# A new hand-written order of issue for the first batch of an attention + gated-product kernel

## Chip, cores and metric

The kernel runs on one core of one Trainium2 chip. The metric is the device time of one execution in microseconds (us); smaller is better. Times are compared between runs of whole programs on the same chip.

## What is computed

Attention over 4 batches, 8 heads, 768 positions and head width 64, with a hash mask, followed by a gated product with three weight matrices. In short:

```python
q_bits = (q @ proj > 0); k_bits = (k @ proj > 0)            # 6 bits each
mask   = bucket(q_bits)[:, :, :, None] == bucket(k_bits)[:, :, None, :]
scores = where(mask, q @ k.T / 8, -1e9)
attn   = exp(scores - max) / (sum(exp) + 1e-9)
x      = (attn @ v)  ->  3072 tokens x 512
out    = ((x @ w_a) * (x @ w_b)) @ w_out                    # 512 -> 1536 -> 512
```

## The kernel before

The numbers keep close to float32 although TensorE is fed float16: each operand is scaled and split into a high and a low float16 part, and products are made of three of the four parts.

**Units.** The work is cut by batch (4), by chunk of 256 query rows (3 per batch), and by half (4 heads each). A unit has 8 query tiles (`qtile`). Each tile is: four score matmuls on TensorE (`scores`, L1004), the row maximum on VectorE (L1016), a width (L1025, VectorE) and a bias (L1032 on ScalarE or L1038 on VectorE), the exponential on ScalarE (L1048), a cast to float16 (L1056 VectorE, L1057 ScalarE or L1058 GpSimd), the residue `e - a` (L1068 GpSimd or L1072 VectorE), a DMA transpose issued by SyncE (L1078), and 18 matmuls with V (`outs`, L1087). After both halves of a chunk the result is normalised, split and turned (`su_end`), and `moe` runs the gated product in 12 blocks: 24 matmuls `ab` (L1285), a copy (L1299), a product (L1307), a cast (L1315 or L1319), a residue (L1327, GpSimd) and 6 matmuls `o` (L1337).

**The first batch** has more to do than the others. While its tiles run, the 9.4 MB of weights are loaded, measured (L617), scaled on ScalarE and packed on VectorE (L540, L548, L555), and split into high and low halves (`hi_lo`: L633 or L634, then L638 on GpSimd or L642 on VectorE). K, Q and V of the batch are scaled and split (`scale_pair`, L734 or L731; `split`, L862 to L883), and some of them are turned by TensorE and evicted (L834, L842, L844).

**The order.** Each operation is a step with a number. For each engine the program order is the order in which the steps stand in one list, `ORDER`, written out by hand; nothing is decided at run time but the waits on semaphores. An engine works through its own steps strictly in that order, and so does SyncE with its DMA issues. A number from 10000 up takes the step in another form, mostly on another engine (the `alt` of the step). A negative number -n stands for n matmuls whose result nobody reads ("warm", L1441, 128x128 by 128x256):

```python
def issue(self, order, fill=None):                          # L367
    for x in order:
        if x < 0:
            fill(-x)
            continue
        which, at = divmod(x, 10000)
        o = self.ops[at]
        (o.alt[which - 1][2] if which else o.fn)()

        for _ in range(n):                                  # in fill(n), L1440
            nc.tensor.matmul(
                warm[0][:, 0, :], lhsT=ident16, rhs=ident16.unsqueeze(1).to_broadcast([P, 2, P]), start=True, stop=True
            )
```

The costs and due times that stand beside the steps are not read when the list is there.

Of the kernel before, what the change touches and what calls it, by code (L numbers as in the profile page):

```python
# [75 lines left out]
def constants():  # L76
# [26 lines left out]
    12, 6, 5, 52, 0, 2, 1, 40, 3, 13, 60, 4, 296, 53, 14, 295, 7, 299, 15, -1, 8, 16, 300, 10017, 273, 41, 19, 277, 9,  # L103
    18, -8, 20, 272, 42, 26, 61, 43, 276, 10, -1, 62, 145, 10021, 11, 411, 63, 64, 410, 45, -6, 22, 66, 309, 23, 159,
    298, -7, 24, 67, 46, 301, 25, 44, 65, 302, 297, 303, -1, 54, 10047, 304, 275, 55, 305, 306, 314, 307, -7, 48, 56,
    308, 57, 49, 274, 58, 279, 313, 59, -7, 50, 10027, 315, 51, 278, 280, 310, -10, 281, 10146, 69, 282, 286, 342,
    283, 147, 78, 70, 346, 290, 341, 148, 284, 345, -3, 28, 425, 149, 29, 30, 150, 68, 71, 79, 31, 151, 80, 72, 10081,
    73, 285, 152, 33, -18, 153, 344, 74, 415, 82, 412, 414, 75, 348, 10160, -3, 87, 154, 83, 88, 76, 355, -3, 96, 84,
    89, 161, 10090, 343, 360, 162, 163, 291, -4, 155, 85, 287, 91, 156, 578, 164, 319, 292, -7, 34, 318, 430, 20092,
    97, 157, 323, 10035, 322, 166, 347, 32, 158, 98, 10099, 189, 100, 349, 93, 413, -9, 36, 416, 350, 417, 77, 288,  # L110
    20101, 94, 351, 167, 418, 579, 37, 102, 352, 419, 38, 10168, 420, 289, 421, 103, 580, 86, 424, 665, 588, 39,
    10165, 10581, 426, 429, -10, 105, 114, 583, 427, 169, 354, 584, 428, 320, 106, 359, 115, -9, 95, 332, 170, 107,
    361, -3, 171, 108, 109, 116, 324, 391, 104, 117, 118, 356, 123, 392, 10110, -1, 132, 431, 387, 293, 388, 10111,
    337, 124, 112, 119, 125, 10126, 133, 127, 325, 294, 120, 311, 422, -18, 190, 134, 10135, 321, 10128, 312, 353,
    121, 136, 191, 141, 192, -9, 199, 10193, 10137, 10129, 316, 200, 201, 138, 130, 194, 393, 326, -9, 113, 432,
    10202, 317, 390, 327, 139, 423, 172, 142, 328, 329, -5, 208, 330, 433, 331, 122, 389, 209, 336, 173, -4, 131, 210,
    333, 10582, 203, 181, 334, 365, 338, -7, 140, 10195, 217, 10335, 369, 211, 212, 218, 368, 196, 339, -5, 585, 174,
    401, 340, -3, 175, 219, 394, 197, 220, 182, 204, 364, 586, 10213, 205, 367, 221, -9, 226, 587, 176, 177, -1, 235,
    214, 179, 183, 227, 143, 357, 228, 180, 229, 230, 358, 184, 206, -9, 198, 236, 244, 237, 10238, 178, 185, 239,
    395, 186, 10187, 378, 188, -6, 253, 10222, 838, 254, 10231, 215, 255, 10223, 383, 144, 232, 406, 224, 10256, 245,  # L120
    -15, 207, 257, 20240, 246, 10247, 371, 248, 233, -3, 589, 370, 241, 10839, 362, -1, 598, 262, 840, 366, 841, -4,
    216, 20249, 590, 250, 372, 242, 599, 591, 10592, 10258, -7, 225, 600, 10601, 10363, 602, 251, 263, 10259, 593, -7,
    234, 843, 10594, 607, 260, 616, 848, 595, 608, -1, 243, 603, 609, 10610, 617, 611, 604, 596, 618, 619, 620, -7,
    252, 612, 625, 10613, 605, 634, 626, 20621, -1, 261, 622, 627, 635, 628, 614, 629, 636, 264, 637, 265, 638, -8,
    597, 630, 925, 643, 266, 631, 623, 639, -3, 606, 644, 652, 842, 632, 645, 646, 647, 10267, 268, 653, 844, 10648,
    -8, 666, 654, 10655, 649, 10640, 656, -1, 269, 667, 661, -1, 373, 270, 615, 668, 374, 10669, 20657, 375, 641, 670,
    -3, 633, 271, 658, 624, 382, 396, 650, 662, 675, 397, 377, 20671, 483, 511, 398, 659, 676, 672, 400, 684, 677,
    484, 678, 405, 379, 679, 384, 435, 485, 685, 693, 20680, 380, 439, 642, 434, 486, 686, 10381, 491, 673, 687, 487,
    688, 694, 488, 490, 438, 385, 402, 702, 399, 695, 386, 492, 489, 10689, 703, 651, 704, 493, 705, 660, 10681, 494,
    497, 696, 697, 495, 376, 682, 10403, 10698, 711, 10690, 706, 498, 404, 663, 691, 707, 712, 845, 449, 436, 496,  # L130
    459, 846, 699, 499, 454, 441, 674, 720, 713, 407, 714, 700, 715, 683, 708, 500, 716, 729, 721, 847, 501, 505, 408,
    722, 664, 717, 730, 692, 458, 731, 504, 462, 10723, 10732, 502, 440, 724, 463, 709, 437, 409, 503, 10725, 442,
    461, 506, 733, 443, 1122, 507, 701, 726, 10508, 718, 514, 738, 444, 445, 446, 448, 739, 509, 447, 515, 727, 20734,
    453, 849, 450, 510, 516, 517, 451, 455, 858, 473, 521, 452, 859, 512, 522, 542, 518, 850, 456, 519, 851, 10513,
    478, 735, 860, 464, 520, 523, 460, 852, 853, 465, 457, 710, 10861, 854, 524, 867, 466, 736, 862, 528, 11123, 855,
    525, 1124, 467, 868, 529, 1125, 526, 869, 468, 863, 719, 1127, 876, 530, 856, 870, 527, 871, 531, 1126, 469, 470,
    532, 1128, 728, 864, 877, 472, 535, 471, 10872, 573, 878, 474, 1098, 737, 879, 880, 865, 885, 873, 482, 536,
    10881, 740, 477, 886, 894, 533, 874, 537, 887, 857, 10882, 475, 534, 538, 883, 888, 10539, 476, 889, 895, 545,
    890, 896, 741, 742, 903, 897, 898, 540, 546, 891, 11099, 904, 866, 746, 1100, 905, 10906, 547, 541, 10743, 892,
    899, 1101, 747, 907, 912, 548, 900, 748, 875, 1102, 549, 552, 543, 10908, 744, 1103, 901, 1129, 909, 913, 914,  # L140
    884, 553, 745, 1130, 915, 916, 550, 544, 910, 926, 1105, 921, 935, 554, 1131, 10917, 551, 555, 927, 918, 560, 928,
    936, 1110, 929, 930, 10556, 893, 922, 833, 931, 557, 559, 937, 919, 479, 938, 939, 944, 10932, 1106, 561, 558,
    940, 10480, 945, 902, 481, 911, 946, 562, 933, 953, 947, 948, 567, 10941, 10949, 566, 10563, 942, 954, 564, 962,
    955, 1104, 10956, 1132, 957, 565, 950, 963, 568, 11111, 920, 569, 971, 964, 10965, 10958, 951, 923, 750, 966, 972,
    570, 749, 973, 924, 974, 571, 975, 10959, 934, 751, 1107, 10967, 1112, 572, 1108, 968, 976, 1113, 1109, 752, 980,
    1114, 977, 756, 1148, 1115, 981, 960, 753, 989, 576, 754, 757, 1133, 577, 574, 952, 982, 10983, 758, 943, 990,
    984, 969, 755, 991, 759, 10985, 10992, 1117, 1149, 978, 993, 986, 10760, 764, 1150, 998, 1118, 763, 999, 1151,
    761, 1134, 1152, 1153, 575, 762, 765, 1135, 10994, 1136, 766, 970, 1138, 995, 1137, 10767, 1158, 1167, 987, 1139,
    770, 1225, 768, 1140, 961, 11116, 771, 1159, 21154, 996, 1168, 1155, 979, 772, 1169, 769, 1160, 11161, 773, 1162,
    1156, 778, 1170, 1171, 21163, 1226, 1119, 774, 988, 11172, 775, 1120, 777, 1164, 1141, 1121, 1227, 1176, 779,  # L150
    1228, 1173, 776, 780, 1165, 1229, 1177, 997, 785, 1178, 11230, 1179, 1174, 1000, 10781, 784, 1001, 782, 1002,
    1157, 786, 783, 1180, 1232, 11181, 1185, 787, 1233, 11231, 1194, 1003, 1093, 1182, 1186, 791, 1006, 1237, 1187,
    788, 1004, 1166, 1183, 792, 789, 11188, 1195, 1189, 1005, 1196, 790, 1007, 1197, 793, 21190, 1198, 1008, 794,
    1203, 798, 11199, 10795, 1204, 796, 1234, 799, 1205, 1200, 1235, 11206, 1184, 1238, 1236, 1207, 1175, 11191, 1142,
    800, 797, 11208, 801, 1192, 1143, 802, 1144, 1209, 1239, 1212, 1146, 1201, 1240, 805, 1241, 803, 1213, 1242, 1210,
    806, 1214, 11215, 1145, 1265, 1216, 1244, 1266, 1147, 807, 1249, 804, 1221, 808, 21217, 1257, 1267, 1193, 809,
    1245, 1218, 1275, 1268, 11269, 812, 1270, 1276, 1243, 1219, 813, 1277, 1284, 11278, 810, 1222, 1279, 11271, 11272,
    1280, 1202, 814, 1285, 1211, 1281, 1273, 1293, 815, 1286, 811, 1250, 1287, 816, 1282, 1288, 1258, 817, 819, 1294,
    21289, 1259, 1295, 11296, 820, 1297, 1260, 1261, 1246, 1298, 1251, 821, 818, 1262, 1263, 822, 823, 1264, 826,
    1247, 824, 1438, 827, 1290, 1252, 1248, 1253, 825, 828, 1299, 1255, 829, 1220, 10830, 1009, 831, 1291, 1223, 1439,  # L160
# [1319 lines left out]
```

## Time and profile before

| what | us |
|---|---|
| median of 3 runs | 923.35 |
| the three runs | 919.8, 923.35, 923.75 |
| span of the profiled execution, first to last instruction | 918.4 |

The page of the profile gives no time for the profiled execution but its span. The runs lie 1.4 to 5.35 us above it; the median lies 4.95 us above.

In the rows further down, PE is TensorE, DVE VectorE, ACT ScalarE, POOL GpSimd, SP SyncE, and SPq the queue from which SyncE issues DMAs. Instructions of one engine can overlap by a little, so that the sum of their durations is somewhat over the engine's busy time.

### The profile page before, as it was taken

The page shows a single profiled execution, that of the slowest core. Times are in us where ns is not written, and L with a number is a line of the kernel's source. Part 1 is how long each engine was busy: PE and PEld are TensorE (multiplying, and loading weights), DVE is VectorE, ACT ScalarE, POOL GpSimd, SP SyncE. Part 2 cuts the span into 40 slices and gives each one's busy share as a digit, 9 for nine tenths or more (in the row PEclk, how much of TensorE's full clock was granted, in tenths as well). Part 3 has the DMA queues.
Part 4 walks back from the last instruction along what each step waited for, and adds up shares of the span by engine and source line. Part 5 has one row for each costly group of instructions (what it writes and reads, how often), then busy time and mean ns, then how long its engine had stood idle before and what let it go on. Part 6 is the DMA issues. An engine that isn't in the chain of part 4 may idle for free.

```text
span 918.4 us, 23592 instructions
## 1 busy us (share of the span) xinstructions
PE 864.2 (94%) x9429; PEld 658.4 (72%) x9429; DVE 681.2 (74%) x1622; ACT 543.9 (59%) x1034; POOL 433.0 (47%) x372
## 2 busy tenths in 40 slices
PE   5667789999999999999999999999999999999998
PEld 4455567667777777777777777777777777777775
DVE  7999999998988778777976757776888863752311
ACT  5989879976554656556645455555566545543222
POOL 1347568745553454453343253573454544462111
PEclk9999999999999999999999999999999999999999
DMA  9799999899999789998969579997899976654000
GB/s 330 222 238 235 191 224 229 163 189 194 175 193 184 144 144 197 185 172 153 176 110 187 107 141 163 151 208 151 154 187 169 156 126 113 130 111 70 1 24 24
DMA packets 435950, 147.40 MB, mean 161 GB/s; under 512 B 407552, under 2 KB 428160, under 8 KB 435840
## 3 DMA queue, kind: packets, MB, share of 16 engines
q1 hardware_dynamic: 435840, 145.89, 81.1%
q8 instruction: 74, 1.21, 0.5%
q14 instruction: 36, 0.29, 0.1%
HBM read 37.85 MB, written 6.29 MB: 48 GB/s over the span
## 4 chain that ended last, share of the span: by engine, by line
PE 73%; DVE 9%; ACT 1%; issue 1%; DMA 1%; SPq 0%; ACTq 0%; DVEq 0%
PE ab L1285 36%; PE o L1337 18%; PE s L1004 10%; PE av L1087 8%; DVE mx L1016 2%; DVE xz L1187 1%; DVE g L1307 1%; DMA at<-a 1%; SPq L823 0%; PE b_k L795 0%; PE b_q L795 0%; DVE x L1126 0%; DVE width L1025 0%; DVE vl L781 0%; PE ps_v L450 0%
## 5 line engine op out<-in xcount | busy, mean ns | idle before, releaser
L1285 PE MATMUL ab<-xT,wab 128*128 128x256 f16 x3456 | 408.2, 273 | 3.0 <-DVE g L1307 1.8
L1285 PEld LDWEIGHTS <-wab 128*128 128x128 f16 x3456 | 333.1, 98 | 56.3 <-issue 4.1
L1068 POOL TENSOR_TENSOR a<-e,a 128x768 f16<-128x768 f32 x137 | 230.5, 1686 | 132.6 <-ACT a L1057 71.8
L1048 ACT ACTIVATE e<-s,bias,width 128x768 f32<-128x768 f32 x192 | 189.9, 989 | 83.2 <-DVE bias L1038 67.2
L1327 POOL TENSOR_TENSOR g<-g,g 128x256 f16<-128x256 f32 x144 | 106.2, 738 | 235.0 <-ACT g L1315 144.0
L1337 PE MATMUL o<-wo,g 128*128 128x512 f16 x864 | 209.3, 379 | 0.4 <-DVE ob L1373 0.4
L1016 DVE TENSOR_REDUCE mx<-s 128x1 f32<-128x768 f32 x192 | 181.6, 949 | 26.6 <-PE s L1004 25.8
L1307 DVE SCALAR_TENSOR_TENSOR g<-ab,wlow,a 128x256 f32<-128x256 f32 x132 | 63.6, 482 | 139.8 <-ACT a L1299 127.4
L1299 ACT ACTIVATE a<-ab,wlow 128x256 f32<-128x256 f32 x132 | 62.1, 471 | 162.8 <-PE ab L1285 161.4
L1087 PEld LDWEIGHTS <-at 128*128 128x128 f16 x3456 | 123.0, 98 | 25.3 <-DMA at<-a 5.6
L1337 PEld LDWEIGHTS <-g 128*128 128x128 f16 x864 | 81.9, 98 | 74.8 <-issue 0.6
L1087 PE MATMUL av<-vh,at 128*128 128x64 f16 x2304 | 126.4, 193 | 5.2 <-DMA at<-a 3.8
L1004 PE MATMUL s<-kTA_k,qTA_q 128*128 128x384 f16 x384 | 93.7, 326 | 18.2 <-ACT e L1048 13.9
L1004 PE MATMUL s<-kTB_k,qTB_q 128*128 128x384 f16 x384 | 93.7, 326 | 0.0
L1058 POOL CAST a<-e 128x768 f16<-128x768 f32 x57 | 51.1, 896 | 64.6 <-ACT e L1048 56.4
L1057 ACT CAST a<-e 128x768 f16<-128x768 f32 x92 | 76.0, 830 | 1.9 <-DMA at<-a 0.4
L1087 PE MATMUL av<-vl,at 128*128 128x64 f16 x1152 | 65.2, 193 | 0.0
L1315 ACT CAST g<-g 128x256 f16<-128x256 f32 x99 | 39.7, 401 | 38.2 <-DVE g L1307 33.0
L1004 PEld LDWEIGHTS <-qTA_q 128*128 128x128 f16 x384 | 34.7, 98 | 38.2 <-issue 20.8
L1032 ACT ACTIVATE bias<-mx,width 128x1 f32<-128x1 f32 x91 | 26.4, 292 | 57.1 <-DVE width L1025 56.9
L1072 DVE TENSOR_TENSOR a<-e,a 128x768 f16<-128x768 f32 x55 | 55.0, 1000 | 4.3 <-ACT a L1057 3.9
L1004 PEld LDWEIGHTS <-qTB_q 128*128 128x128 f16 x384 | 37.5, 98 | 24.9
(150 smaller groups left out, 851.9 us busy)
## 6 DMA issues: line engine op xcount, KB each, us to landing
rk_k<-in_k_dram SPq DMA_DIRECT2D x16, 384.0 KB, 4.0
vr<-in_v_dram SPq DMA_DIRECT2D x16, 384.0 KB, 3.9
rq_q<-in_q_dram SPq DMA_DIRECT2D x12, 512.0 KB, 4.7
raw_w<-in_moe_w_b_dram SPq DMA_DIRECT2D x12, 512.0 KB, 5.9
raw_w<-in_moe_w_a_dram SPq DMA_DIRECT2D x12, 512.0 KB, 7.1
raw_wo<-in_moe_w_out_dram SPq DMA_DIRECT2D x12, 512.0 KB, 4.9
out_dram<-ob SPq DMA_DIRECT2D x24, 256.0 KB, 2.8
at<-a SPq DMA_TRANSPOSE x192, 4.1
```

Source lines behind the costliest of these rows:

```text
L1004: nc.tensor.matmul(ps.t[:, jj, :HALF], lhsT=x.t[:, uq, :], rhs=y.t[:, h * NT + jj * 3 : h * NT + jj * 3 + 3, :].rearrange("p t x -> p (t x)"),
L1016: lambda: nc.vector.tensor_reduce(out=mx.t[:, u : u + 1], in_=halves(ps.t), axis=AX.XY, op=ALU.max, negate=True),
L1048: lambda: nc.scalar.activation(flat2(e.t), halves(ps.t), AF.Exp, bias=bias.t[:, u : u + 1], scale=width.t[:, u : u + 1], accum_out=sm.t[:, ...
L1057: ("ACT", 0.725, lambda: nc.scalar.copy(out=a2.t[:, 0], in_=e.t), False),
L1068: lambda: nc.gpsimd.tensor_tensor(out=a2.t[:, 1], in0=e.t, in1=a2.t[:, 0], op=ALU.subtract),
L1072: lambda: nc.vector.tensor_tensor(out=a2.t[:, 1], in0=e.t, in1=a2.t[:, 0], op=ALU.subtract), True,
L1087: nc.tensor.matmul(av.t[:, u, :], lhsT=at.t[:, a + kt, :], rhs=w.t[:, h, kt, :], start=i == 0, stop=i == 3 * NT - 1,)
L1285: nc.tensor.matmul(pl.t[:, m, :CH], lhsT=wt(m, wi, cc, f), rhs=xt.t[:, :, xi * NC + cc, :], start=i == 0, stop=i == 3 * NC - 1,)
L1299: lambda a=a, pl=pl, gr=gr: nc.scalar.activation(a.t, pl.t[:, 0, :CH], AF.Copy, scale=cuts[:, gr : gr + 1]),
L1307: lambda a=a, g32=g32, pl=pl, gr=gr: nc.vector.scalar_tensor_tensor(out=g32.t, in0=pl.t[:, 1, :CH], scalar=cuts[:, gr + 1 : gr + 2], in1=a ...
L1327: lambda g=g, g32=g32: nc.gpsimd.tensor_tensor(out=g[1].t, in0=g32.t, in1=g[0].t, op=ALU.subtract),
L1337: nc.tensor.matmul(po.t[:, u, :], lhsT=g[gi].t[:, us], rhs=wo[f // 2].t[:, f % 2, wi * DM : (wi + 1) * DM], start=f % per_q == 0 and i == ...
```

## The change

Only `ORDER` is different. Both lists hold the same 3677 steps, and their last 2438 entries are the same. The first 1286 entries of the old list (1239 steps and 47 runs of warm matmuls, 273 in all) become 1277 entries (the same 1239 steps, 38 runs, 305 warm matmuls). The longest runs were 18, 18 and 15; they are now 26, 23, 22, 22 and 20. All warm matmuls are in both lists ahead of the first `ab` of chunk (0,0).

Steps have also changed engine. Step 1112 serves here as a mark: it is the small matmul at L450 that spreads the maximum of K of batch 1, pair 1, over the partitions, and it stands shortly before the score matmuls at the end of batch 0. These are the steps that must have been done by each engine when step 1112 can start: its own predecessors, theirs, and all that stands ahead of them in each engine's own order.

| engine | steps ahead of 1112, old list | new list | what differs (old to new) |
|---|---|---|---|
| VectorE | 333 | 317 | residues L1072 11 to 4; the five instructions of `one_scale` (L1246 to L1252) 1 to 0; casts L634 2 to 0; L642 3 to 2; L943 2 to 1; L1208 1 to 0; smaller ones |
| ScalarE | 204 | 210 | casts L633 16 to 18; casts L1057 27 to 28; L937 2 to 3; L769 3 to 4; L862 of K one more; smaller ones |
| GpSimd | 76 | 80 | residues L1068 31 to 37; L874 of Q 3 to 1; smaller ones |
| SyncE | 104 | 104 | one transpose of `a` fewer, one load of K or V more |
| TensorE | 164 | 162 | one `o`, one `av` and one K bucket group fewer, one L450 more; warm matmuls 273 to 305 |

```diff
 ORDER = [
-    12, 6, 5, 52, 0, 2, 1, 40, 3, 13, 60, 4, 296, 53, 14, 295, 7, 299, 15, -1, 8, 16, 300, 10017, 273, 41, 19, 277, 9,
-    18, -8, 20, 272, 42, 26, 61, 43, 276, 10, -1, 62, 145, 10021, 11, 411, 63, 64, 410, 45, -6, 22, 66, 309, 23, 159,
-    298, -7, 24, 67, 46, 301, 25, 44, 65, 302, 297, 303, -1, 54, 10047, 304, 275, 55, 305, 306, 314, 307, -7, 48, 56,
...
-    570, 749, 973, 924, 974, 571, 975, 10959, 934, 751, 1107, 10967, 1112, 572, 1108, 968, 976, 1113, 1109, 752, 980,
...
+    5, 6, 4, 12, 52, 0, 3, 2, 60, 1, 40, 13, 300, 299, 53, 14, 26, 296, 15, 295, 16, 273, 61, 17, 277, 145, 7, 276,
+    62, 19, 272, 41, 18, 8, 9, 20, 410, 10, 11, 10021, 42, 63, 64, 43, 22, 65, 23, 314, 45, -6, 24, 66, 302, -1, 46,
...
+    285, 151, 68, 286, 152, -23, 153, 315, 425, 578, 71, 10160, 284, 345, 154, 31, -8, 161, 10072, 162, -1, 78, 73,
...
+    321, 136, 192, 324, 294, 193, 320, -26, 199, 194, 325, 122, 10137, 588, 326, 327, 583, 427, 171, 141, 138, 200,
...
+    571, 1112, 922, 751, 565, 1136, 950, 1113, 1138, 923, 1107, 10974, 752, 20958, 572, 951, 975, 1114, 1108, 1109,
...
```

## Rows read from the trace of the kernel before

**Rows 1.** Page, part 2: 40 slices of the span, TensorE and VectorE.

```profile
PE   5667789999999999999999999999999999999998
DVE  7999999998988778777976757776888863752311
```

**Rows 2.** Busy us by stretch: PE, PEld, DVE, ACT, POOL; clock, DMA share, GB/s.

```profile
0.00:20.00 20.00, 10.68 (x91) 8.62 (x92) 14.62 (x41) 10.41 (x10) 3.09 (x7) 1.00 0.90 320
...
0.00:208.30 208.30, 160.63 (x1872) 123.09 (x1872) 194.17 (x464) 175.10 (x271) 118.31 (x83) 0.98 0.98 224
20.00:100.00 80.00, 55.64 (x635) 42.52 (x634) 77.18 (x195) 76.03 (x104) 42.88 (x26) 0.96 0.95 237
100.00:180.00 80.00, 69.03 (x851) 53.05 (x848) 75.38 (x179) 68.35 (x117) 59.73 (x41) 1.00 1.02 204
180.00:208.30 28.30, 25.28 (x305) 18.90 (x304) 26.99 (x52) 20.30 (x43) 12.61 (x10) 1.00 0.99 177
208.30:283.00 74.70, 74.53 (x823) 56.77 (x820) 64.62 (x165) 42.85 (x85) 39.20 (x34) 1.00 0.98 183
283.00:918.40 635.40, 629.02 (x6742) 478.54 (x6740) 422.37 (x994) 325.99 (x680) 275.51 (x256) 1.00 0.75 137
```

**Rows 3.** Waits of TensorE's matmuls after 208 us: us, times, longest.

```profile
PE ab L1285 <- DVE g L1307: 0.2, 1, 0.2
...
PE ab L1285 <- DVE g L1307: 1.2, 1, 1.2
PE av L1087 <- DMA at<-a: 0.4, 1, 0.4
```

**Rows 4.** Timeline around step 1112 (the L450 row): start, length, instruction.

```profile
206.94 1.20 DVE L1072 TENSOR_TENSOR a<-e,a 128x768 f16<-128x768 f32 x1
208.06 0.55 DVE L1056 CAST a<-e 128x768 f16<-128x768 f32 x1
...
202.36 1.46 PE L1337 MATMUL o<-wo,g 128*128 128x512 f16 x6
208.27 0.47 PE L450 MATMUL ps_k<-ident,mx_k 128*128 128x128 f32 x2
```

**Rows 5.** VectorE instructions that move; the first row gives shortest, median, longest ns.

```profile
L1072 DVE TENSOR_TENSOR a<-e,a x12: 907/950/2347, 64.3 to 206.9; 128x768 f16<-128x768 f32 x12
...
L642 DVE TENSOR_TENSOR wab<-wab 128x1024 f16<-128x1024 f32 x3 | 3.7, 1220 | 0.3 <-ACT wab L633 0.3
L943 DVE TENSOR_REDUCE qmx_q<-rq_q 128x1 f32<-128x1024 f32 x2 | 2.4, 1208 | 0.0
L1208 DVE TENSOR_TENSOR x<-x,xsc 128x512 f32<-128x512 f32 x1 | 1.3, 1269 | 0.0
L1250 DVE TENSOR_SCALAR wlow<-wone,wtop 128x3 f32<-128x3 f32 x1 | 1.2, 1225 | 0.0
L634 DVE CAST wab<-wab 128x1024 f16<-128x1024 f32 x1 | 0.7, 683 | 0.0
```

**Rows 6.** ScalarE: its waits up to 208 us, and two kinds of cast.

```profile
ACT bias L1032 <- DVE width L1025: 8.9, 7, 2.4
ACT nB_q L937 <- DMA rq_q<-in_q_dram: 6.1, 1, 6.1
ACT e L1048 <- DVE bias L1038: 4.9, 6, 1.3
...
L633 ACT CAST wab<-wab 128x1024 f16<-128x1024 f32 x10 | 10.5, 1046 | 0.0
L1057 ACT CAST a<-e 128x768 f16<-128x768 f32 x32 | 26.2, 829 | 0.7 <-DMA at<-a 0.4
```

**Rows 7.** GpSimd's residues up to 208 us.

```profile
L1068 POOL TENSOR_TENSOR a<-e,a 128x768 f16<-128x768 f32 x32 | 55.6, 1740 | 23.9 <-ACT a L1057 21.1 <-DVE ks_k L470 2.0 <-PE s L1004 0.2
```

**Rows 8.** One run of 18 warm matmuls in TensorE's timeline.

```profile
29.90 2.13 PE L1441 MATMUL warm<-ident 128*128 128x256 f16 x18
```

**Rows 9.** Stretches where the granted clock is below 1; columns as in rows 2.

```profile
44.00:48.00 4.00, 0.92 (x17) 0.62 (x14) 3.96 (x9) 1.87 (x2) 1.98 (x2) 1.00 1.14 350
48.00:52.00 4.00, 3.88 (x45) 3.80 (x45) 3.40 (x15) 3.85 (x6) 2.62 (x3) 0.58 1.19 375
```

**Rows 10.** SyncE's queue: eleven DMA transposes in a row.

```profile
93.94 23.95 SPq L1078 DMA_TRANSPOSE at<-a  x11
```

376 rows, old and new, of the table ORDER are left out of this document.

## Prediction, made before the changed kernel was run

> **What bounds the kernel now.** I first read the slices of the page. TensorE's digit climbs from 5 to 9 over the first seven slices, some 160 us, and stays at 9 nearly to the end; VectorE stands at 9 for that time and falls off behind it [rows 1]. So there are two regimes, and the change is in the first. Next come the sums by stretch [rows 2]. From 208.3 us to the end TensorE is busy 74.53 of 74.70 and 629.02 of 635.40 us. Before that it is busy only 160.63 of 208.3 us, 47.7 us idle. VectorE is busy 77.18 of 80 us from 20 to 100, 75.38 of 80 to 180, 26.99 of 28.3 after; ScalarE 76.03, 68.35 and 20.30. Over the first 208.3 us VectorE idles 14.1 us and ScalarE 33.2 us. So in the front VectorE sets the pace, with ScalarE close behind, and nearly level with it up to 100 us. Third, the waits: behind 208 us the longest waits of TensorE's matmuls are 1.2, 0.4 and 0.2 us, each once [rows 3]. The tail is TensorE's own work, in the same order in both lists. Hence the sum: what the new order saves before TensorE is full is saved at the end, one to one, and nothing else counts.
>
> I measure the front at step 1112, which TensorE starts at 208.27 us [rows 4]; by then it has no more gaps.
>
> **VectorE's part.** Ahead of step 1112 the new list has fewer VectorE instructions. Seven residues fewer (L1072): 7 x 0.950 = 6.7 us. The five instructions of `one_scale`, whose longest is 1.225 us, and which last 2.3 us together, come later. Two casts L634 x 0.683 = 1.4. One each of L642, L943 and L1208: 1.22 + 1.21 + 1.27 = 3.7 [rows 5]. That makes 14.1; some ten other kinds, none changing by more than 0.94 us, give a net 1.6 more. Total 15.7 us. Instructions of an engine overlap by some 0.08 us (the residue at 206.94 ends at 208.14, the cast behind it starts at 208.06, [rows 4]), so that is about 1 us too much; I keep 15.7 as the far end.
>
> **ScalarE's part.** It gets more: two casts L633 x 1.046 = 2.1, one cast L1057 0.83 [rows 6], and a further Q sum, V scaling, K scaling and x piece, less one L1114 and one L1032, 3.8 together: 6.7 us.
>
> **GpSimd's part.** Six residues more, 6 x 1.740 = 10.4 [rows 7], two copies of Q fewer and smaller ones: about +7.7 us. It was busy 118.31 of 208.3 us [rows 2], so this has 90 us of idle time to lie in. If that cover fails, each moved residue reaches its transpose 1.740 - 0.950 = 0.8 us later, 4.7 us for six; but a transpose waits in SyncE's queue and has slack, so I take nothing.
>
> The rows show how VectorE's residues fare beside GpSimd: the shortest takes 0.907, the median 0.950, the longest 2.347 us [rows 5]. The Trainium skill, in "SBUF — State Buffer", section "Who interferes with whom", says that a VectorE instruction with two SBUF inputs and a GpSimd one that reads SBUF exclude each other for a whole instruction. That speaks against moving work from the one to the other; this trace agrees in so far as a residue can last 1.44 us longer than the shortest. By that page alone six more residues on GpSimd could take back 6 x 1.44 = 8.6 us; by the median, 0.04 us over the shortest, it is 0.3 us. I take the median.
>
> **TensorE's part.** At step 1112 the new list has done one `o` (1.3 us, the next group starts 1.29 us after the row at 202.36, [rows 4]), one `av` (0.52) and one bucket group (0.3) less, and one L450 (0.2) more: 1.9 us of useful work is still to be done after the mark. That is a loss of 1.9.
>
> The warm matmuls rise by 32. Eighteen take 2.13 us, the last one's latency included, so about 0.107 each [rows 8]: 3.4 us. They all come early, where TensorE is idle 24.4 of 80 us even with the old warm runs counted as busy [rows 2]; I take 0, with 3.4 if the cover is gone.
>
> The clock: after 4 us with only 0.92 us of TensorE work, the grant falls, to a mean of 0.58 in the next 4 us [rows 9], which means it spent most of them at 1.2 GHz, the lower of its two levels. Warm matmuls in the gaps may prevent that. In that stretch 4 x 0.42 = 1.7 us of clock is lost, but VectorE was busy 3.40 of the 4 us, so at most 0.6 us was on its account. Bounds 0 and 1.7; I take 0.
>
> **SyncE's part.** The same number of issues stands ahead of the mark; one transpose fewer, one load more. Transposes go through at up to 24/11 = 2.2 us each [rows 10]; some 50 ahead of the mark make 110 us of 208. No bound, 0. Blocks of transposes standing elsewhere in the list may free or delay a load, below.
>
> **The sum.** Two ends. If VectorE alone sets the front and idles as before, the mark comes at 208.3 - 15.7 = 192.6, less the 1.9: 13.8 us gained. If ScalarE sets it and still idles 33.2 us, it comes 6.7 later, and with the 1.9 the kernel loses 8.6 us. Between them I go by the stretches. ScalarE's idle time is 9.6 us before 20 us, of which 6.1 is the wait for Q's load [rows 6], and 4.0 from 20 to 100 us: I keep these 13.6. The other 19.6 us come after 100 us, where its waits name VectorE: 8.9 for widths, 4.9 for biases [rows 6]. These shrink when VectorE sheds work; I take off the whole 15.7, which leaves 3.9. That is 4% of the 108 us from 100 to 208.3, near the 4.0 of 80 (5%) that ScalarE shows from 20 to 100: it can run that full beside a full VectorE. So ScalarE reaches the mark at 175.1 + 6.7 + 13.6 + 3.9 = 199.3 us, 9.0 earlier; less 1.9 is 7.1; rounded down, as two engines both near full wait for each other more, 7.0. Span 918.4 - 7.0 = 911.4. The runs' median lies 4.95 us above that span, and nothing outside it changes: 916.4 us.
>
> **Rivals.**
> 1. *VectorE alone decides* (ScalarE's waits vanish): 13.8 us, 909.6. For it: VectorE is the fullest engine in every stretch up to 208 us. Against: ScalarE has 175.1 + 6.7 us to do in 194.
> 2. *ScalarE takes its place, slower than before.* Place: the exponentials and casts of batch 0 between 100 and 208 us. Price: +6.7 of work with 33.2 idle unchanged, and the 1.9: 8.6 us, 932. It decides once ScalarE's idle time up to the mark stays over 29 us (208.3 + 4.6 - 1.9 - 181.8); at 24.6 it has eaten the whole gain. Against: its waits after 100 us are mostly for VectorE.
> 3. *The port between VectorE and GpSimd.* Six residues more on GpSimd hold up VectorE's two-input instructions by the 1.44 us seen at worst: 8.6 us of the 7.0 gained, 925, no measurable change.
> 4. *The order doesn't do what it says, or the gain is lost on the way.* Warm runs of 20 to 26 (2.1 to 2.8 us) hold a score group that is ready; five of them cost up to 12.1 us, with half on the path 6. Or, in the tail, a transpose comes late, as the 0.4 us wait shows it can, for a TensorE that is now 7 us earlier. Gain 0 to 2, 922. Against: the waits shown for the tail come to 1.8 us in 710.
>
> **Chances.** About 0.5% (4.6 us) is what a measurement of this kernel can tell from no change. My forecast, 3 to 11 us gained (912.4 to 920.4): 0.45, of it 0.38 beyond 4.6. Rival 1 and more, 11 to 17 gained: 0.17. Rival 2, 0.13, nearly all of it beyond +4.6. Rival 3, 0.12 and rival 4, 0.13, most of it within the bound. Faster 0.38 + 0.17 + 0.01 = 0.56; same 0.30; slower 0.14. The range goes from 17.3 us gained (906: rival 1, and the clock and warm terms on the good side) to 928, half way into rival 2; some 0.15 is left outside. The forecast's own range is 912 to 920.
>
> **What would show it.** Right: TensorE's slices reach 9 one slice earlier or so; its idle time up to the mark falls from 47.7 us by about 10; step 1112 starts near 199 us; ScalarE is busy over 90% up to the mark, and the waits for widths and biases shrink. VectorE's L1072 count drops by some 7 before the mark and its median stays near 0.95. After the mark TensorE waits no more than 2 us. Wrong: ScalarE idle over 25 us up to the mark (rival 2); L1072 and other two-input instructions with a mean far above before (rival 3); score groups that start as a warm run ends (rival 4); or new waits of `av` for transposes after 200 us.

## The result, and the profile after

The changed kernel takes 929.91 us (median of 4 runs, 929.12 to 930.05), the kernel before 921.69 beside it: ratio 1.0095, 95% interval 1.0071 to 1.0118. The forecast was 916.4, faster; it is slower, and just outside the range. The profiled span is 928.2 us, 9.8 more than before. Line numbers of the changed kernel are those of the front plus 3 (L1004 is now L1007, L1087 is L1090); in most experiments they are the front's minus 3 (L1001, L1084), in the mirror image minus 2.

The page's slices of the changed kernel, to be read against [rows 1]:

```profile
PE   5867797989999999999999999999999999999998
DVE  7989797988687877877977756867898964752311
PEclk9998999999999999999999999999999999999999
```

TensorE starts better (8 for 6 in slice two, 9 for 8 in slice six), then dips to 7 in slice seven and 8 in slice nine, where it stood at 9; VectorE's long row of nines is gone. The busy time by stretch, columns as in [rows 2], with one stretch up to step 1112, which now starts at 209.96 us (208.27 before):

```profile
0.00:208.30 208.30, 164.83 (x1854) 124.40 (x1855) 183.50 (x439) 175.19 (x270) 128.46 (x89) 0.96 0.94 220
20.00:100.00 80.00, 61.34 (x699) 46.48 (x698) 74.57 (x173) 70.45 (x103) 47.48 (x30) 0.94 0.88 221
100.00:180.00 80.00, 67.39 (x761) 50.09 (x760) 68.78 (x169) 68.37 (x115) 59.75 (x39) 0.96 0.95 204
...
208.30:283.00 74.70, 71.30 (x787) 53.90 (x786) 58.44 (x158) 45.92 (x91) 41.29 (x36) 0.98 1.01 181
...
0.00:210.00 210.00, 166.53 (x1870) 125.94 (x1871) 185.09 (x443) 176.65 (x273) 130.16 (x90) 0.96 0.94 220
```

VectorE is busy 9.1 us less by the mark (185.09 against 194.17; 15.7 were counted), and idles 24.9 us instead of 14.1. ScalarE idles 33.4 us, as before (33.2). So no engine is full any more, and the mark comes 1.7 us later instead of 9 earlier. What VectorE waits for, from 58 to 210 us, first before, then after (us, times, longest):

```profile
DVE g L1307 <- ACT a L1299: 1.7, 5, 0.4
DVE wo_y L555 <- ACT raw_wo L540: 0.8, 1, 0.8
DVE mx L1016 <- PE s L1004: 0.3, 1, 0.3
```

```profile
DVE mx L1019 <- PE s L1007: 5.0, 4, 3.3
DVE b_q L807 <- PE b_q L798: 2.3, 1, 2.3
DVE al_wo L581 <- PE ps_wo L575: 1.5, 1, 1.5
```

It waits for TensorE, which before it hardly ever did. And TensorE, up to 300 us, waits longer for transposes:

```profile
PE s L1007 <- ACT e L1051: 9.3, 13, 1.9
PE av L1090 <- DMA at<-a: 8.8, 8, 2.8
...
PE ps_v L453 <- DVE mx_v L737: 5.2, 2, 3.0
PE b_q L798 <- DMA qTB_q<-nB_q: 3.0, 1, 3.0
PE s L1007 <- DMA kTA_k<-marked: 2.1, 1, 2.1
```

The three DMA rows and 0.8 us for `kTB_k` make 14.7 us; before it was the `av` row alone (the first row, waits for ScalarE, was 13.6 us before):

```profile
PE av L1087 <- DMA at<-a: 3.4, 4, 1.3
```

One of these waits, in SyncE's queue and then in TensorE's timeline (start, length, instruction, idle time before):

```profile
54.78 1.98 SPq L522 DMA_DIRECT2D raw_w<-in_moe_w_a_dram  x3
57.46 7.17 SPq L1081 DMA_TRANSPOSE at<-a  x2
```

```profile
62.24 0.49 PE L1007 MATMUL s<-kTB_k,qTB_q 128*128 128x384 f16 x2
65.52 0.35 PE L1090 MATMUL av<-vh,at 128*128 128x64 f16 x6 [2.79 <-DMA at<-a]
```

The transpose is issued at 57.46 behind three weight loads of 512 KB and is there at 65.5; `av` (step 122) stands in TensorE's list ahead of work that is ready, and holds it up. After each such wait the granted clock falls to the lower of its two levels (columns as in [rows 9]):

```profile
66.80:70.20 3.40, 3.40 (x20) 2.28 (x18) 2.61 (x5) 2.77 (x4) 1.56 (x1) 0.51 1.13 213
77.10:83.90 6.80, 5.02 (x19) 3.02 (x20) 6.34 (x16) 5.90 (x9) 3.76 (x3) 0.50 1.00 235
...
152.20:155.60 3.40, 3.30 (x35) 2.55 (x36) 1.88 (x9) 0.09 (x1) 3.21 (x2) 0.50 1.13 377
237.50:240.90 3.40, 3.40 (x28) 2.36 (x27) 2.46 (x10) 0.70 (x1) 2.91 (x3) 0.50 1.10 217
```

With one more at 111.2 that is 20.4 us at half clock, at most 10.2 lost; before it was 6.8 us, at most 3.4 lost. The waits ahead of these stretches begin at 62.7, 75.9, 109.0, 149.3 and 234.3 us. The Trainium skill, "TensorE: Matmul & The Clock Gate", section "HAM oscillation — how this bites in real kernels", describes the like: a kernel that waits for DMAs between bursts starts each burst at the lower clock. This trace agrees in kind, at four waits of 2.1 to 3.0 us for DMAs and at one for VectorE; the waits of that section are longer, 3 to 5 us.

**Where the time went.** I add up TensorE's steps along its list, without warm runs, and compare when the same sum is done. At 21 us of useful work the changed kernel is 10 us ahead (58.1 against 68.6 us), the peak of a lead that is mostly 5 to 8 us around it. It loses 5 of these by 81 us, 4 more by 115, 5 by 158 and 6 by 246; from then on it is 9.4 us behind, nearly unchanged to the end. Waits for landing DMAs (+11.3 us) and half clock (at most +6.8) make 18.1 of the 19.6 us so lost. This is a count along one engine and not yet a cause; over the same part, warm matmuls take 4.7 us more and waits for ScalarE 4.3 us less, and these two about cancel.

### The profile page after: what moved, and what is told of

The parts are those of the page before. It is cut to its first block, busy times and chain, and to the rows that moved or that the text cites. A ratio compares the mean times of both kernels' runs of the same rounds, so it can differ in the third digit from the quotient of the medians.

```text
span 928.2 us, 23652 instructions
## 1 busy us (share of the span) xinstructions
PE 874.7 (94%) x9461; PEld 663.7 (72%) x9461; DVE 674.1 (73%) x1600; ACT 551.3 (59%) x1049; POOL 447.3 (48%) x382
## 4 chain that ended last, share of the span: by engine, by line
PE 70%; DVE 8%; DMA 4%; ACT 2%; issue 2%; POOL 0%; ACTq 0%; DVEq 0%; SPq 0%; POOLq 0%
PE ab L1288 34%; PE o L1340 17%; PE s L1007 9%; PE av L1090 8%; DVE mx L1019 2%; DMA at<-a 2%; DVE xz L1190 1%; DMA qTB_q<-nB_q 1%; DMA kTB_k<-nB_k 1%; DVE g L1310 1%; DMA kTA_k<-marked 1%; ACT e L1051 1%; DVE vl L784 0%; DVE width L1028 0%; PE b_q L798 0%
## 5 line engine op out<-in xcount | busy, mean ns | idle before, releaser
L1071 POOL TENSOR_TENSOR a<-e,a 128x768 f16<-128x768 f32 x144 | 246.0, 1711 | 116.4 <-ACT a L1060 58.4
L1019 DVE TENSOR_REDUCE mx<-s 128x1 f32<-128x768 f32 x192 | 181.6, 949 | 33.8 <-PE s L1007 33.2
L1090 PEld LDWEIGHTS <-at 128*128 128x128 f16 x3456 | 123.3, 98 | 30.4 <-DMA at<-a 12.1
L1090 PE MATMUL av<-vh,at 128*128 128x64 f16 x2304 | 126.6, 194 | 9.1 <-DMA at<-a 8.8
L1007 PE MATMUL s<-kTA_k,qTA_q 128*128 128x384 f16 x384 | 95.5, 331 | 12.7 <-ACT e L1051 9.7
L1007 PE MATMUL s<-kTB_k,qTB_q 128*128 128x384 f16 x384 | 95.2, 330 | 0.0
L1090 PE MATMUL av<-vl,at 128*128 128x64 f16 x1152 | 65.4, 193 | 0.0
L1007 PEld LDWEIGHTS <-qTA_q 128*128 128x128 f16 x384 | 35.1, 99 | 32.1 <-issue 14.1
L1007 PEld LDWEIGHTS <-qTB_q 128*128 128x128 f16 x384 | 38.0, 99 | 26.0 <-issue 1.7
L1075 DVE TENSOR_TENSOR a<-e,a 128x768 f16<-128x768 f32 x48 | 47.7, 994 | 4.5 <-ACT a L1060 3.9
```

The source lines that it names most:

```text
L1007: nc.tensor.matmul(ps.t[:, jj, :HALF], lhsT=x.t[:, uq, :], rhs=y.t[:, h * NT + jj * 3 : h * NT + jj * 3 + 3, :].rearrange("p t x -> p (t x)"),
L1019: lambda: nc.vector.tensor_reduce(out=mx.t[:, u : u + 1], in_=halves(ps.t), axis=AX.XY, op=ALU.max, negate=True),
L1071: lambda: nc.gpsimd.tensor_tensor(out=a2.t[:, 1], in0=e.t, in1=a2.t[:, 0], op=ALU.subtract),
L1090: nc.tensor.matmul(av.t[:, u, :], lhsT=at.t[:, a + kt, :], rhs=w.t[:, h, kt, :], start=i == 0, stop=i == 3 * NT - 1,)
```

## Experiments

"After" is 929.9 us (1.0095); before is measured again beside each group, 920.3 to 920.7. The diffs show only the steps around an edit, not whole lines of the list.

**1. Order and engines taken apart.** 120 steps changed engine. One kernel has the new list with every step on its old engine, another the old list with every step on its new one:

```diff
-    16, 273, 61, 17, 277, 145,      (new list; 17 is on ScalarE)
+    16, 273, 61, 10017, 277, 145,   (its old form, on VectorE)
```

> The changed order with every step on the engine on which the old list had it (the old forms at the new places). Engine-move theory (GpSimd's added residues hold up VectorE): the loss goes, 921 to 924 us. Late-transpose theory: the waits for transposes stay or move and VectorE has some 15 us more to do, so no better than 929 and up to 938 us.

> The list of the kernel before, place by place (its 273 warm matmuls too), but each of the 120 steps whose engine the change moved is done by the engine that the change gave it. Theory A (the moves of engine gain, the new places lose): it is the first experiment's complement. The new list with the old engines took 945.3 us, 15 us more than with the new ones; on the old places the moves should gain something of that size, though the old places were planned for the old engines: 906 to 918 us. Rival (an engine moved only pays at the place planned for it, so the two can't be told apart): 925 us or more. Rival (the moved residues and bias sums make transposes late, and that is the loss): about 930, as the changed kernel.

New places, old engines: 945.27 us, 1.0260 [1.0237, 1.0282]. Old places, new engines: 939.08 us, 1.0214 [1.0189, 1.0238]. So at the new places the new engines are worth 15.4 us; at the old places they cost 18.8. Neither half gains by itself: an engine is right for a place. The theory that the moves gain in any case fell.

**2. The named waits taken away.** Six steps of TensorE moved later (122, 175, 261, 597, 845, 1185); then, in the list as it was, eight loads of SyncE moved behind the transposes:

```diff
-    194, 325, 122, 10137, 588,
+    194, 325, 10137, 588,
...
-    142, -9, 208, 201,
+    142, -9, 122, 208, 201,
```

> The changed order with six TensorE steps put a little later, so that TensorE has other work where it now waits 2 to 3 us for a transpose or a scale: `av` 122, the V scale 175, `av` 261 and 597, the Q bucket group 845, the score group 1185. Late-transpose theory (TensorE's list asks for transposes before they land, and each wait is followed by a stretch at half clock): these five waits come to some 13 us, about 10 of it can be filled, so 920 to 925 us. Engine-move theory and warm-matmul theory: nothing that they name is touched, 929 to 931 us.

> The changed kernel, with eight ordinary loads on SyncE's queue issued behind the transposes that they stood ahead of: the weight loads 318, 322 and 323 (with the eight small steps that wait for them) behind load 181, 364 and 369 behind transpose 260, 365 behind 605, 458 behind 844, and K's load 1237 behind 1121. No TensorE step moves. Theory A1 (the late transposes are late because loads ahead of them hold the queues): av 122, av 597, b_q 845 and the scores at 1185 wait 1 to 2 us less each, with less half clock behind them: 920 to 926 us. Theory A2 (TensorE's steps stand too early for their transposes, and the loads only decide which one is late): other waits take their place, 927 to 932 us.

The first: 927.97 us (ten runs from 923.5 to 935.1), 1.0078 [1.0050, 1.0106], about 2 us better, if anything. The second: 932.29, 1.0131 [1.0116, 1.0146], no gain. In the first the waits for transposes fall, but the scores wait instead, for VectorE (3.7 us once) and for ScalarE to free their PSUM buffers:

```profile
PE s L1001 <- ACT e L1045: 10.9, 13, 2.7
PE av L1084 <- DMA at<-a: 5.4, 9, 1.0
...
PE s L1001 <- DVE marked L805: 3.7, 1, 3.7
```

In the second the wait of step 122 is gone, but that of 597 grows from 2.4 to 3.6 us, most others stay, and the sums are no smaller:

```profile
PE s L1001 <- ACT e L1045: 14.5, 14, 3.9
PE av L1084 <- DMA at<-a: 8.7, 8, 3.6
```

So the loads decide which transpose is late, not how much is lost.

**3. Warm matmuls.** All taken out, of the new list and of the old one; and 87 put into four real waits of the new list (26 ahead of step 122, 28 of 175, 11 of 261, 22 of 597):

```diff
-    194, 325, 122, 10137,
+    194, 325, -26, 122, 10137,
```

> The changed order without any of its 305 warm matmuls. Warm theory (runs of 20 to 26 hold up score groups): faster than 927 us. Late-transpose theory: the waits stay and the clock falls more often, slower than 930 us.

> The kernel before without its 273 warm matmuls. Taking 305 away from the changed kernel cost 3.6 us. If the warm runs stand where they are needed in the old list, it loses as much or more: 924 to 928 us. If the old list has little idle time in which the clock falls in any case, 921 to 923. Faster than before would mean that the warm runs hold up work that is ready.

> The changed order with 87 more warm matmuls in the real waits (26 before step 122, 28 before 175, 11 before 261, 22 before 597): the waits stay as long, but TensorE is not idle in them. If the half clock behind each wait is what costs, three of the five slow stretches go, up to 6.8 us: 923 to 927 us. If only the waits themselves cost, 929 to 931 us. If warm matmuls themselves cost (warm theory), up to 939 us.

Without: 933.52 us, 1.0128 [1.0096, 1.0160] for the new list, 921.56 us, 1.0011 [0.9998, 1.0025] for the old. Warm runs are worth some 3 us to the new list and 1 to the old, neither clear of the intervals; without them the orders differ by no less (12 us), so the 32 extra ones are not the loss. Up to 210 us the granted clock is then 0.80 in the new list (0.96 with them) and 0.85 in the old (0.98): much more half clock, with the matmuls that nobody reads saved, costs little. With the 87: 926.98 us, 1.0069 [1.0046, 1.0092], the best of the new list, with two stretches at half clock instead of five; some 2.5 us come back, though the intervals overlap.

**4. VectorE's port.** In the window from 73 to 78 us two of VectorE's instructions take far longer than elsewhere (timeline of the changed kernel, VectorE and then GpSimd):

```profile
72.95 2.63 DVE L558 SCALAR_TENSOR_TENSOR wab<-raw_w 128x1024 int32<-128x1024 int32 x1
75.51 2.34 DVE L881 COPY marked<-nB_q 128x1024 f16<-128x1024 f16 x1
```

```profile
72.86 1.64 POOL L1071 TENSOR_TENSOR a<-e,a 128x768 f16<-128x768 f32 x1 [4.50 <-ACT a L1060]
74.46 3.10 POOL L641 TENSOR_TENSOR wab<-wab 128x1024 f16<-128x1024 f32 x1
```

Elsewhere they take 1.22 and 0.42. I moved the second of these GpSimd steps (312, L641) behind the residue 214, and then put warm matmuls into three waits besides:

```diff
-    586, 332, 312, 175, 197,
+    586, 332, 175, 197,
...
-    236, 214, -4, 198,
+    236, 214, 312, -4, 198,
```

> The changed kernel with one GpSimd step moved: the subtraction 312 (L641 on wab, 3.10 us from 74.46 us, beside VectorE's L558 that took 2.63 in place of 1.22 us and its copy L881 that took 2.34 in place of 0.42) goes behind the residue 214 in the list. No other engine's steps move. Theory P (the port collision of rival 3 decided that window): VectorE gets 2 to 3 us back there, the wait of 3.03 us at 75.85 us shrinks to under 1 and the half clock behind it (6.8 us long, 3.4 us lost) goes: 924 to 927 us. Theory T (the late transposes and the first-come order of TensorE's list decide; VectorE's delay is made good in its later idle time): 928 to 931.

> The same, and warm matmuls in three real waits (26 ahead of step 122, 11 ahead of 261, 22 ahead of 597), so that the half clock behind them goes as well. With 28 more ahead of 175 and without the move of 312 it was 927.0 us. If the waits of 58 to 120 us and the half clock behind them are what the change loses, the lead of 10 us at 58 us is kept in good part: 918 to 922 us. If other waits take their place, 925 to 929.

931.02 us (1.0116 [1.0099, 1.0133]) and 931.48 (1.0123 [1.0108, 1.0138]): nothing back. The copy is at 0.41 again, L558 (here L552) is not. It began just behind the residue (L1071, here L1065) in both kernels, so for it the step that I moved was the wrong one. TensorE's `av` steps now wait 10.0 us for transposes, 8.8 in the changed kernel:

```profile
74.88 2.64 DVE L552 SCALAR_TENSOR_TENSOR wab<-raw_w 128x1024 int32<-128x1024 int32 x1
77.44 0.41 DVE L875 COPY marked<-nB_q 128x1024 f16<-128x1024 f16 x1
```

```profile
74.80 1.65 POOL L1065 TENSOR_TENSOR a<-e,a 128x768 f16<-128x768 f32 x1 [5.64 <-ACT a L1054]
```

**5. Several mends together.** Parts of 2, 3 and 4 in one list (`e11`: 312, three warm runs, 845 to 847 and 1185; `e8`: four warm runs and five loads):

```diff
-    441, 10725, 845, 699, 514,
+    441, 10725, 699, 514,
```

> The same, and TensorE's b_q steps 845 to 847 behind step 683 and its scores 1185 behind 769, so that the waits of 2.96 us at 149 and 2.05 us at 234 us go too. All the named losses are mended here: by their sum (16 us of the 19 found) 914 to 920 us, faster than before. If waits move on to the next step instead, 924 to 928 us.

> The changed kernel with warm matmuls in four of its real waits (26 ahead of step 122, 28 ahead of 175, 11 ahead of 261, 11 ahead of 597) and with the loads 364, 365, 369, 458 and 1237 behind the transposes that they stood ahead of. The warm matmuls alone gave 927.0 us. If the loads ahead of transposes cost 1 to 2 us each at 109, 149 and 234 us, and the half clock behind the last two goes as well (1.7 us each), 919 to 923 us; if the loads only decide which transpose is late, 926 to 929.

929.08 us, 1.0098 [1.0083, 1.0113], and 930.50, 1.0113 [1.0095, 1.0131]. Both have far less half clock than the changed kernel's 20.4 us (10.2 in `e11` and 6.8 in `e8`; 10.2 too in the second list of experiment 4, 931.48 us), and none is faster, so the clock alone is not the loss. In `e11` the `av` waits are longer than in the changed kernel, in part at other steps:

```profile
PE av L1084 <- DMA at<-a: 12.6, 13, 2.5
PE s L1001 <- ACT e L1045: 8.6, 8, 3.4
```

**6. The mirror image.** In the kernel before, five `av` moved earlier, ahead of ready work and ahead of their transposes; then the same with 76 warm matmuls in four of the waits:

```diff
-    192, -9, 199, 10193,
+    192, -9, 113, 199, 10193,
...
-    326, -9, 113, 432, 10202,
+    326, -9, 432, 10202,
```

> The mirror image, in the kernel before: five av steps are moved earlier in TensorE's list, ahead of work that is ready, to where by the old trace their transposes land 2 to 2.6 us later (113 ahead of the scores 199, 252 ahead of 607, 624 ahead of 652, 651 ahead of the bucket group 483, 1166 ahead of 784). Nothing else moves; the five av are only done earlier. 11.6 us of waits in all. If TensorE's idle time of 47.7 us in the front takes such waits in, 920 to 923 us. If a wait of TensorE for a transpose goes to the end one to one, because it holds up the scores that feed VectorE and ScalarE, and half a clock of 3.4 us follows each: 930 to 940 us.

> The kernel before with the five early av steps of the mirror image (933.5 us), and warm matmuls in the waits ahead of four of them (20 ahead of 113 and 252, 18 ahead of 624 and 651), so that the clock stays up behind them. If the half clock makes a good third of such a wait's price, 927 to 930 us; if it is the wait alone, 933 or more.

933.54 us, 1.0141 [1.0120, 1.0162]: 12.9 us for five steps moved. Its waits, TensorE's for `at` and VectorE's for scores (58 to 285 us; 0.8 us before):

```profile
PE av L1085 <- DMA at<-a: 15.9, 8, 3.0
```

```profile
DVE mx L1014 <- PE s L1002: 12.0, 9, 3.2
```

12.5 us more of waits for transposes, 12.9 us more of time, with VectorE now waiting for the scores held up behind `av`. TensorE's idle time did not take them in. That the two numbers agree is a net result: half clock rose too, from 6.8 to 27 us, and TensorE's waits for ScalarE fell from 13.6 to 7.0. With warm matmuls in the waits it is 929.98 us, 1.0087 [1.0059, 1.0115]; half clock went from 27 to 14 us, and some 4 of the 12.9 us came back. So here a good quarter of the price of such a wait was the clock behind it.

**7. The tight steps moved later, all of them.** If the waits are the loss, every `av` with little slack should go later: 22 steps with less than 1 us, or 36 with less than 3 us, together with the moves of 845 to 847 and 1185 and 28 warm matmuls ahead of 175 (some 2.5 and 3 us later each); and in the old list its 12.

```diff
-    323, 170, 113, 293, 426,
+    323, 170, 293, 426,
...
-    320, -26, 199, 194,
+    320, -26, 113, 104, 199, 194,
```

> The changed kernel with the 22 av steps whose transposes land less than 1 us ahead of TensorE's arrival, or behind it, moved some 2.5 us of TensorE's list later (step by step by its own trace, up to 285 us); nothing else moves. Theory L (TensorE's list as a whole stands too early for the transposes): the waits for transposes fall from 20 to under 10 us and the loss with them, 918 to 924 us. Theory M (waits move on to others): 927 to 932 us.

> The changed kernel with all 36 av steps of less than 3 us of slack moved some 3 us later, b_q 845 to 847 and the scores 1185 moved later as in the earlier runs, and 28 warm matmuls ahead of step 175. Theory L: 914 to 921 us. Theory M: 925 us or more, with PSUM buffers and at buffers that come free later as the next wait.

> The kernel before with its 12 av steps of less than 1 us of slack (all between 72 and 116 us) moved some 2.5 us later in TensorE's list. Theory L: its 9.3 us of waits for transposes shrink by half and it gains 2 to 5 us, 916 to 919 us. Theory M: the scores that now go ahead find no free PSUM buffer, 920 to 924 us.

930.54 us, 1.0095 [1.0060, 1.0129]; 939.69, 1.0188 [1.0162, 1.0214]; and for the old list 925.65, 1.0045 [1.0028, 1.0063], slower too. In the first:

```profile
PE s L1001 <- ACT e L1045: 12.1, 14, 1.7
...
PE av L1084 <- DMA at<-a: 5.3, 5, 2.3
PE b_q L792 <- DMA qTB_q<-nB_q: 3.6, 1, 3.6
```

`av` waits 3.5 us less, the scores 2.8 us more. The theory that TensorE's list merely stands too early for the transposes fell: less waiting for them brought no time.

**8. Is VectorE's work still the price, and is the clock?** The 21 residues of the new list back on their old engines; and 92 warm matmuls in eight real waits of the old list.

```diff
-    -1, 350, 111, 103, 421,
+    -1, 350, 10111, 103, 421,
```

> The changed kernel with the 21 residues whose engine the change moved (14 from VectorE to GpSimd, 7 the other way) done by their old engines; every place and every other engine stays. VectorE gets 7 x 0.95 = 6.7 us of work more, GpSimd 7 x 1.74 = 12.2 less. The prediction's main term (VectorE sets the pace of the front, its work goes into the time one to one): 935 to 938 us. If VectorE's work is covered by its idle time of 25 us in the front: 928 to 932 us. If GpSimd's late residues and its use of VectorE's memory port are the loss: 922 to 927 us.

> The kernel before, its order untouched, with 92 more warm matmuls in eight of TensorE's real waits from 44 to 103 us (11, 14, 9, 10, 15, 12, 11 and 10 of them ahead of steps 36, 350, 105, 171, 190, 585, 589 and 234). Its two stretches at half clock (48 and 82 us, 3.4 us each, 3.4 us lost) should go. If the clock is worth what it was in the changed kernel: 917 to 920 us, the fastest of all kernels here. If TensorE's clock has cover in VectorE's pace there, 920 to 922; above that, the warm runs hold up ready work.

932.98 us, 1.0136 [1.0121, 1.0151]: 3 to 4 us for 6.7 us of VectorE's work, so half of it finds cover. The front's busy times (VectorE 185.09 to 188.10, GpSimd 130.16 to 115.27 us), and VectorE's L558 up to 210 us (count, then us in all and mean ns):

```profile
0.00:210.00 210.00, 166.29 (x1860) 126.02 (x1861) 188.10 (x443) 175.84 (x269) 115.27 (x80) 0.98 0.94 219
```

```profile
L552 DVE SCALAR_TENSOR_TENSOR wab<-raw_w 128x1024 int32<-128x1024 int32 x11 | 18.1, 1654 | 0.0
```

Old list with the warm matmuls: 919.90 us, 0.9995 [0.9984, 1.0007]. The clock is 1.0 throughout, and nothing is gained: there the half clock had cover.

## Why the prediction was wrong

**The step that failed** is the last of the sum: "These shrink when VectorE sheds work; I take off the whole 15.7, which leaves 3.9". I summed each engine's work and kept or shrank its idle time. The idle time did not stay: VectorE's rose by 10.8 us, ScalarE's stayed at 33.4. 9.1 us less work and 10.8 us more idle time is the mark 1.7 us later. Two terms put at nothing go with it. One is "SyncE's part ... No bound, 0": I asked whether SyncE has time enough, not when a transpose lands against the place of its `av`, and TensorE came to wait 11.3 us longer for landing DMAs. Rival 4 had a late transpose only in the tail, and only for the gain. The mirror image shows that such waits can cost about their length, the clock behind them included. The other is the port between VectorE and GpSimd, taken by the median at 0.3 us and left out of the sum: two lines of VectorE (below) lost 7.9 us by it, and of the 15.7 us counted off VectorE 9.1 showed in its busy time.

**What held.** The undone 1.9 us of TensorE's work: at the mark the kernel is 1.7 + 1.9 = 3.6 us behind. That the tail runs the same: from 283 us on hardly anything more is lost. That the old kernel's half clock costs next to nothing (experiment 8). It is chance that the new engines are worth 15.4 us at the new places, near the 15.7 counted: in that experiment all 120 moves went back, not VectorE's alone, and experiment 8 found 3 to 4 us for 6.7 us of VectorE's work.

**What else was off.** "Nothing else counts" after the mark: 3.4 us idle and a clock of 0.98 from 208.3 to 283 us, where it was 0.17 us and 1.00. The clock, taken as 0 to 1.7 us in the front's favour, costs TensorE 6.8 us more by my count; the fills of experiment 3 gave perhaps 2.5 back, those of experiments 4 and 5 nothing. The warm runs, a loss in rival 4, are worth some 3 us, if anything.

**The rivals.** Rival 2 comes near in time (932) by chance. Its condition is met, ScalarE idle over 29 us, but its cause is not: ScalarE's busy time by the mark rose by 1.6 us, not 6.7, and it waits for TensorE and VectorE. Rival 3 is seen in the rows, by another route than I gave it. Up to 210 us, after (before: 13.3 us and 1221 ns for the first):

```profile
L558 DVE SCALAR_TENSOR_TENSOR wab<-raw_w 128x1024 int32<-128x1024 int32 x11 | 18.0, 1635 | 0.0
...
L881 DVE COPY marked<-nB_q 128x1024 f16<-128x1024 f16 x3 | 4.5, 1509 | 0.0
```

These two lines lose 4.7 and 3.2 us. Of the 4.7, 2.4 fall beside two residues that are GpSimd's in both lists (from 42.45 and 72.86 us), 1.4 beside L641 and 0.6 beside a copy (L877). With the moved residues back on VectorE L558 takes 18.1 us all the same, at other steps. So in this row it is the new places that collide, not the six residues. And one collision taken away gave nothing. The Trainium skill, "SBUF — State Buffer", section "Who interferes with whom", names both kinds, two SBUF inputs and copies in a two-port mode, as contending with GpSimd, and says of the second that whoever issues first keeps the port for a whole instruction. The 2.34 us of a copy that takes 0.42 alone agrees.

**What stays open.** Which property of the new list costs the 25 us that it loses against the old one on the same engines (experiment 1). Waits for transposes and the clock behind them account for 18 of the 19.6 us lost after the lead, and the mirror image shows that they can cause such a loss; but no mend of up to 36 steps gave back more than 3 us, since the next step then waits, for another transpose, for a PSUM buffer or for VectorE. Six results (the new places with the old engines, the loads moved, the second list of experiment 4, both of 5, the old list of 7) were slower than every range set down for them, by 0.3 to 7.3 us, so the account by waits does not foretell what its own mends do. That the waits are the first cause is argued, not shown. No version tried beats the kernel before by more than its measurement can tell.

## What to carry to other kernels

A front in which no engine is full is not bounded by the sums of its engines; take from the fullest engine only what its neighbours can deliver in time, and for each consumer of a DMA compare the landing with its place in the engine's list. A wait of an in-order engine ahead of ready work can cost about its length in full; in the mirror image 12.5 us of them on TensorE cost 12.9, a good quarter of which was the clock behind them. When a change moves places and engines at once, measure the two apart early: here each half alone was over 2% slower than the kernel before.

## What the runs showed of the hardware

A 128x1024 float16 copy on VectorE took 0.42 us alone and 2.34 us beside a GpSimd subtraction. The two-input instruction L558 took 2.25 and 2.63 us where a GpSimd residue had begun before it (42.45 and 72.86 us), but 1.22 us where the residue began after it (54.80, L558 from 54.72); there the residue took 2.63 us instead of 1.64. A transpose issued behind three loads of 512 KB on the same queue was there 8.0 us after its issue (57.46 to 65.5), one issued at 53.21 after 3.8; with the loads behind the transposes, others were late. The granted clock fell after single waits of 2.1 to 3.0 us, with work on both sides of them; around the first, from 60 to 66 us, TensorE was busy 2.27 us.
